# Output rows in token order, half chunks joined, and all output transfers small and on one queue

## The chip, the cores and the metric

The kernel runs on one core of a Trainium2 chip. A core has a matrix engine (TensorE, PE in the profile, with its weight loads as PEld), a vector engine (VectorE, DVE), a scalar engine (ScalarE, ACT), a general engine (GpSimd, POOL) and SyncE (SP), which here only issues transfers. Products land in PSUM; all other on-chip data lie in SBUF, 128 partitions wide. The metric is the device time of one launch in microseconds.

## What is computed

Linear attention with exponential features, then a layer that mixes the first 64 Fourier modes along the sequence, and a residual with a channel product:

```python
q, k, v: (8, 8, 576, 64);  w_phi: (64, 128)
def phi(x):
    proj = x @ w_phi
    proj = proj - max(abs(proj), axis=-1)
    return concat([exp(proj), exp(-proj)])
num = phi(q) @ (phi(k)^T v);  den = phi(q) . sum_s phi(k) + 1e-6
x = (num / den) as (8, 576, 512)                  # heads side by side

X = rfft(x, axis=1)[:, :64]
Y = X @ (w_r + i w_i)                             # per mode a 512 x 512 matrix
y = irfft(Y, n=576, axis=1)
u = x + y
out = u + relu(u @ w_ch)                          # float32
```

## The kernel before

**Tokens.** The 576 tokens of a batch are read as p and n, token = 9 p + n with 64 values of p and 9 of n. The kernel keeps them in five chunks c: partition 64 jj + p of chunk c holds token n = 5 jj + c, with jj = 0 or 1. Chunk 4 has only jj = 0, so half of its 128 rows mean nothing. The attention result x is xs_all, one 128x512 block per batch and chunk, index i = 5 b + c.

**Two stages.** The first (up to L605) runs the attention, 32 steps, and beside it the mode products as their weights arrive: 32 groups k of 8 modes by 128 rows (the first eight cut otherwise), two loads each, wr and wi, of which three groups' buffers exist (pool pw, tags w0 and w1). The last ten groups, k = 22 to 31, run after the attention, in the loop of L685. The loads are issued by GpSimd, each when the buffer of three groups earlier is free.

In that loop a group does mode_mm (L382), mode_sum (L416), a transpose (ptY) into sY, and for every second group by_batch (L660): from sY it makes z = Y w_ch (psZ, PSUM tag T0) and a reordered Y (psR, tag T1) for 32 of the 128 mode rows. Four copies per by_batch then spread both over zall and yall by batch (copy(j), L676: batches j and j + 4; ScalarE for zall, VectorE for yall). They are queued in the list copies and taken out one by one between other work. pieces(n) (L648) fills in n times: flip_x transposes two blocks of xs_all (tag T3) into sT, times_w multiplies them by w_ch (tag T2) and ScalarE casts the result into xw. plan gives n for each k.

**The output units.** After the last group 20 units follow (L738 to L775). A unit is two blocks: two chunks of one batch, or chunk 4 of batches b and b + 4. chan (L710) adds xw through an identity and the inverse transform CI times zall in PSUM, and ScalarE takes the relu into the output tile. spec (L721) does CI times yall; VectorE adds it to the tile. The residual xs_all comes in either through one more identity product (ident_b), or, where a unit is called late, through an addition on GpSimd (L736). Eleven units are late: the four of chunk 4, and seven of the eight with chunks 0 and 1. Chunks and units go by batch: b and b + 4 for b = 0 to 3; for b = 3 the unit of chunk 4 comes first.

PSUM has four tags of two banks, T0 to T3. Units 0, 1 and 2 and all even units use T2 (chan) and T3 (spec), the others T0 and T1, which are free once the last by_batch's copies are done.

**Transfers.** For b < 3 an output tile of[x] leaves when its four chunks are done, as two transfers of 512 KB, partitions 0 to 63 (jj = 0) by SyncE and 64 to 127 (jj = 1) by ScalarE's queue two or three units later; for b = 3 there are two of 256 KB per unit. Chunk 4 leaves from partitions 0 to 63 of Yacc, one transfer of 256 KB in rows of 2 KB. That is 24 transfers, 9.44 MB.

The order on every engine is the order of the code (tc.manual_schedule), and each engine works through its own in sequence.

Of the kernel before, what the change touches and what calls it, by code (L numbers as in the profile page):

```python
# [10 lines left out]
F32 = mybir.dt.float32  # L11
F32R = mybir.dt.float32r
BF16 = mybir.dt.bfloat16
I32 = mybir.dt.int32
ACT = mybir.ActivationFunctionType
ALU = mybir.AluOpType
# [4 lines left out]
DMODEL = 512  # L21
NCH = 5
# [4 lines left out]
def kernel(  # L27
# [11 lines left out]
    nc = tc.nc  # L39

    const = ctx.enter_context(tc.tile_pool(name="const", bufs=1))
    pers = ctx.enter_context(tc.tile_pool(name="pers", bufs=1))
    psum_cm = tc.tile_pool(name="psum", bufs=1, space=bass.MemoryType.PSUM)
    psum = psum_cm.__enter__()
    pw = ctx.enter_context(tc.tile_pool(name="pw", bufs=3))

    ident_b = const.tile([128, 128], BF16, name="ident_b")

    XT1 = pers.tile([128, 80, NMODES], BF16, name="XT1")
    xs_all = pers.tile([128, B_ * NCH, DMODEL], BF16, name="xs_all")

    Yacc = pers.tile([128, 8, DMODEL], F32, name="Yacc")
# [7 lines left out]
    CI = const.tile([128, NCH, 128], BF16, name="CI")  # L62
# [9 lines left out]
    coefcol = pa_c.tile([128, 1], F32, name="coefcol")  # L72
# [420 lines left out]
    def inverse_matrix(c):  # L493


        if c == 0:
            make_identity(nc, ident_f)
            nc.vector.memset(coefcol, 2.0 / S_)
            nc.vector.memset(coefcol[0:2, :], 0.0)
            nc.vector.memset(coefcol[0:1, :], 1.0 / S_)  # L500
        pct = psum.tile([128, 128], F32, name="pct", tag="tx", bufs=1)
        nc.tensor.transpose(pct, trig[:, c, :, :].rearrange("p m r -> p (m r)"), ident_f)
        nc.vector.tensor_scalar_mul(out=CI[:, c, :], in0=pct, scalar1=coefcol)

    psY = None
    k_in = k_out = 0
# [2 lines left out]
    with tc.manual_schedule():  # L509
# [15 lines left out]
        for n in range(N + 2):  # L525
# [60 lines left out]
            e = n - (N + 2 - N_EARLY)  # L586
# [10 lines left out]
            if 10 <= n < 10 + NCH:  # L597
                inverse_matrix(n - 10)
# [16 lines left out]
    psum = ctx.enter_context(tc.tile_pool(name="psumT", bufs=1, space=bass.MemoryType.PSUM))  # L615
# [4 lines left out]
    yall = pb.tile([128, B_, DMODEL], BF16, name="yall", bufs=1)  # L620
    zall = pb.tile([128, B_, DMODEL], BF16, name="zall", bufs=1)
# [3 lines left out]
    todo = list(range(N_EARLY, B_ * NCH, 2))  # L625
    ahead = []
    copies = []
# [20 lines left out]
    def pieces(n):  # L648
        for _ in range(n):
            if todo:  # L650
                flip_x(todo.pop(0))
            if copies:
                copies.pop(0)()
            if len(ahead) > 1:
                times_w()
            if copies:
                copies.pop(0)()


    def by_batch(sY, P):  # L660
        cols = [sY[:, dc].rearrange("p g c -> p (g c)") for dc in range(4)]
        psZ = psum.tile([128, 2, DMODEL], F32, name="psZ", tag="T0")
        for h in range(2):
            for dc in range(4):
                for j in range(4):
                    nc.tensor.matmul(psZ[32 * j:32 * j + 32, h, :], lhsT=cols[dc][:, j + 4 * h::8],
                                     rhs=wchb[:, dc, :], start=(dc == 0), stop=(dc == 3))
        psR = psum.tile([128, 2, DMODEL], F32, name="psR", tag="T1")
        for h in range(2):
            for dc in range(4):  # L670
                for j in range(4):
                    nc.tensor.matmul(
                        psR[32 * j:32 * j + 32, h, dc * 128:(dc + 1) * 128],
                        lhsT=cols[dc][:, j + 4 * h::8], rhs=ident_b, start=True, stop=True)

        def copy(j):  # L676
            r = slice(32 * j, 32 * j + 32)
            nc.scalar.copy(zall[32 * P:32 * P + 32, j::4, :], psZ[r])
            nc.vector.tensor_copy(yall[32 * P:32 * P + 32, j::4, :], psR[r])

        copies.extend([lambda j=j: copy(j) for j in range(4)])

    with tc.manual_schedule():
        plan = {22: 3, 23: 3, 24: 2, 25: 2, 26: 2, 27: 1, 28: 2, 29: 1, 30: 1, 31: 0}
        while k_out < 32:  # L685
            k = k_out
            gi = groups[k][1]
            while k_in < min(k_out + NW, 32):
                weights(k_in)
                k_in += 1  # L690
            yst = mode_sum(k, mode_mm(k, "T3"), pb)
            k_out += 1
            if yst is not None:
                if ahead:
                    times_w()
                pt = psum.tile([128, 4, 128], BF16, name="ptY", tag="T3")
                for dc in range(4):
                    nc.tensor.transpose(pt[:, dc, :], yst[:, dc * 128:(dc + 1) * 128], ident_b)
                if gi % 2 == 0:
                    sY = pb.tile([128, 4, 2, 128], BF16, name="sY", tag="sY")  # L700
                nc.vector.tensor_copy(sY[:, :, gi % 2, :], pt)
                if gi % 2 == 1:
                    by_batch(sY, gi // 2)
            pieces(plan[k])
            if k == 30:
                times_w()
        assert not todo and not ahead and len(copies) == 4


    def chan(u):  # L710
        ps = psum.tile([128, 2, DMODEL], F32, name="psB", tag=u["tags"][0])
        for x, (b, c) in enumerate(u["bc"]):
            i = b * NCH + c
            nc.tensor.matmul(ps[:, x, :], lhsT=ident_b,  # L714
                             rhs=xw0[:, i, :] if i < N_EARLY else xw[:, i - N_EARLY, :],
                             start=True, stop=False)
            nc.tensor.matmul(ps[:, x, :], lhsT=CI[:, c, :], rhs=zall[:, b, :],  # L717
                             start=False, stop=True)
        nc.scalar.activation(u["o"], ps, ACT.Relu)

    def spec(u):  # L721
        ps = psum.tile([128, 2, DMODEL], F32, name="psA", tag=u["tags"][1])
        for x, (b, c) in enumerate(u["bc"]):
            i = b * NCH + c
            if not u["late"]:
                nc.tensor.matmul(ps[:, x, :], lhsT=ident_b, rhs=xs_all[:, i, :],
                                 start=True, stop=False)
            nc.tensor.matmul(ps[:, x, :], lhsT=CI[:, c, :], rhs=yall[:, b, :],  # L728
                             start=u["late"], stop=True)
        o = u["o"]  # L730
        nc.vector.tensor_tensor(out=o, in0=ps, in1=o, op=ALU.add)  # L731
        if u["late"]:
            (b, c), (b1, c1) = u["bc"]
            i0 = b * NCH + c
            di = b1 * NCH + c1 - i0
            nc.gpsimd.tensor_tensor(out=o, in0=o, in1=xs_all[:, i0:i0 + di + 1:di, :], op=ALU.add)  # L736

    units = []  # L738
    for b in range(4):
        last = b == 3  # L740
        of = [pw.tile([128, 4, DMODEL], F32, name="of", tag=f"w{x}") for x in range(2)]
        o4 = Yacc[:, 2 * b:2 * b + 2, :]
        us = []
        for x in range(2):
            out_v = out[b + 4 * x].rearrange("(p n) e -> p n e", n=9)
            for c in (0, 2):
                dmas = []
                if last or c == 2:
                    c0 = c if last else 0
                    dmas = [(out_v[:, 5 * jj + c0:5 * jj + c + 2, :],  # L750
                             of[x][64 * jj:64 * jj + 64, c0:c + 2, :]) for jj in range(2)]
                us.append(dict(bc=((b + 4 * x, c), (b + 4 * x, c + 1)), o=of[x][:, c:c + 2, :],
                               late=c == 0 and not (last and x == 1), dmas=dmas))
        u4 = dict(bc=((b, 4), (b + 4, 4)), o=o4, late=True,
                  dmas=[(out[b::4].rearrange("x (p n) e -> p x n e", n=9)[:, :, 4, :], o4[0:64])])
        units += [u4] + us if last else us + [u4]

    with tc.manual_schedule():

        LAG = 3  # L760
        copies.pop(0)()
        for n in range(len(units) + LAG):
            if copies:
                copies.pop(0)()
            if n < len(units):
                u = units[n]
                u["tags"] = ("T2", "T3") if n % 2 == 0 or n < 3 else ("T0", "T1")
                chan(u)
                spec(u)
                for dst, src in u["dmas"][0:1]:  # L770
                    nc.sync.dma_start(dst, src)
            for lag, late in ((2, False), (3, True)):
                if 0 <= n - lag < len(units) and units[n - lag]["late"] == late:
                    for dst, src in units[n - lag]["dmas"][1:2]:
                        nc.scalar.dma_start(dst, src)  # L775


# [28 lines left out]
```

## Time and profile before

| | |
|---|---|
| median of three runs | 466.02 us (464.96 to 467.11) |
| the profiled execution | 464.41 us, of which the profile's span is 462.6 |
| PE, DVE, ACT, POOL busy | 306.8, 300.0, 255.6, 199.0 us |
| issue of the last weight load (wi) | before 387.69 us, used by PE at 415.48 |
| first and last output transfer issued on SP | 427.02 and 457.0 us |
| last add on DVE | 453.29 to 454.51 us |
| output transfers on SP | 10 from of, 467 / 494 / 1367 ns to issue (least, median, most); 4 from Yacc, 621 / 622 / 647 |
| output transfers on ACT's queue | 10, 474 / 506 / 812 ns |
| relu (ACT), add (DVE), residual add (POOL) of a unit | 1.02, 1.22 and 2.13 us |

Times in the profile are microseconds from the start of the span. A line of the order of instructions has start, duration, engine, source line, operation, what it writes and reads, and in brackets how long the engine had been idle and for whom. A line of the stage windows has busy time and number of instructions for PE, PEld, DVE, ACT and POOL, then the granted clock of PE as a share of full, the DMA engines' share and their rate in GB/s. SPq and ACTq are the issues of transfers on SyncE and ScalarE.

### The profile page before, as it was taken

The page shows a single profiled execution, that of the slowest core. Times are in us where ns is not written, and L with a number is a line of the kernel's source. Part 1 is how long each engine was busy: PE and PEld are TensorE (multiplying, and loading weights), DVE is VectorE, ACT ScalarE, POOL GpSimd, SP SyncE. Part 2 cuts the span into 40 slices and gives each one's busy share as a digit, 9 for nine tenths or more (in the row PEclk, how much of TensorE's full clock was granted, in tenths as well). Part 3 has the DMA queues.
Part 4 walks back from the last instruction along what each step waited for, and adds up shares of the span by engine and source line. Part 5 has one row for each costly group of instructions (what it writes and reads, how often), then busy time and mean ns, then how long its engine had stood idle before and what let it go on. Part 6 is the DMA issues. An engine that isn't in the chain of part 4 may idle for free.

```text
span 462.6 us, 11028 instructions
## 1 busy us (share of the span) xinstructions
PE 306.8 (66%) x4598; PEld 203.3 (44%) x4615; DVE 300.0 (65%) x417; ACT 255.6 (55%) x519; POOL 199.0 (43%) x247
## 2 busy tenths in 40 slices
PE   1575777655677686656465655666577887577991
PEld 1364665543454565534343443444344444333440
DVE  5678789854988788866555564765333456437882
ACT  3765786743676877755555453656122434336671
POOL 4596486545564356644344333433021131001782
PEclk9997798976787859997677787998999999979997
DMA  8999999999999999999999999999999999970997
GB/s 189 252 249 246 245 185 218 228 206 222 216 226 219 229 218 229 218 227 221 218 208 228 208 218 219 208 206 209 206 207 207 207 207 207 207 133 1 232 317 269
DMA packets 83553, 99.08 MB, mean 214 GB/s; under 512 B 3248, under 2 KB 75568, under 8 KB 82736
## 3 DMA queue, kind: packets, MB, share of 16 engines
q0 software_dynamic: 73872, 74.72, 97.1%
q1 hardware_dynamic: 8672, 19.40, 14.0%
q10 hardware_dynamic: 960, 4.26, 2.9%
q8 instruction: 36, 0.59, 0.5%
q14 instruction: 13, 0.11, 0.1%
HBM read 163.64 MB, written 9.44 MB: 374 GB/s over the span
## 4 chain that ended last, share of the span: by engine, by line
DMA 32%; DVE 22%; issue 19%; PE 14%; POOL 5%; ACT 4%; SPq 1%; DVEq 0%; ACTq 0%; POOLq 0%
DMA wi<-in_moe_w_i_dram 19%; DVE mkq L225 7%; DMA wr<-in_moe_w_r_dram 7%; DMA q<-in_q_dram 4%; DVE xs_all L328 4%; DVE nd L314 3%; DVE tB L307 3%; DMA kn<-in_k_dram 2%; PE ptr L176 2%; ACT AA L232 2%; PE psNB L297 2%; PE psB L714 2%; PE psA L728 2%; PE psB L717 2%; POOL vaug L262 2%
## 5 line engine op out<-in xcount | busy, mean ns | idle before, releaser
L262 POOL TENSOR_TENSOR vaug<-vn,ee 128x576 bf16<-128x576 f32 x64 | 72.6, 1152 | 59.7 <-ACT ee L247 53.1
L232 ACT ACTIVATE AA<-psT 128x1024 bf16<-128x1024 f32 x64 | 62.0, 1021 | 44.4 <-PE psT L200 43.9
L154 POOL DMA_DIRECT2D wr<-in_moe_w_r_dram x24 | 21.8, 908 | 111.4 <-PE psY L408 105.5
L254 ACT ACTIVATE e<-mkq 64x4 f32<-64x4 f32 (+1 forms) x128 | 26.3, 206 | 66.1 <-DVE mkq L225 61.8
L236 ACT ACTIVATE AA<-psk 128x1024 bf16<-128x1024 f32 x64 | 61.3, 1008 | 0.0
L408 PE MATMUL psY<-wi,XT 128*32 128x512 bf16 x192 | 24.2, 452 | 31.3 <-DMA wi<-in_moe_w_i_dram 31.3
L646 ACT CAST xw<-psW 128x1024 bf16<-128x1024 f32 x17 | 17.2, 1012 | 48.1 <-PE psW L644 48.1
L408 PEld LDWEIGHTS <-XT 128*32 128x32 bf16 x384 | 17.9, 167 | 57.5 <-issue 49.7
L225 DVE TENSOR_REDUCE mkq<-psk 128x8 f32<-128x1024 f32 x32 | 38.7, 1211 | 0.7 <-PE psk L191 0.7
L225 DVE TENSOR_REDUCE mkq<-psq 128x8 f32<-128x1024 f32 x32 | 38.9, 1216 | 0.2
L427 DVE TENSOR_TENSOR Yacc<-psY,Yacc 128x512 f32<-128x512 f32 x16 | 11.0, 688 | 41.7 <-PE psY L408 41.7
L644 PE MATMUL psW<-wchb,sT 128*128 128x512 bf16 x127 | 33.2, 393 | 3.7 <-ACT xw L646 2.1
L278 PE MATMUL kvz<-vaug,AA 64*128 64x65 bf16 x1152 | 30.4, 214 | 6.3 <-POOL vaug L267 5.1
L182 DVE COPY kT<-ptr 128x640 bf16<-128x640 bf16 x32 | 15.7, 491 | 29.1 <-PE ptr L176 29.1
L408 PE MATMUL psY<-wr,XT 128*32 128x512 bf16 x192 | 23.8, 451 | 16.1 <-DMA wr<-in_moe_w_r_dram 6.3
L307 DVE TENSOR_TENSOR tB<-psNB,e 128x650 f32<-128x650 f32 x32 | 26.7, 833 | 10.9 <-PE psNB L297 10.3
L297 PEld LDWEIGHTS <-AA 128*128 128x128 bf16 x640 | 30.4, 113 | 7.6 <-issue 6.9
L328 DVE TENSOR_TENSOR xs_all<-nd,rden 128x640 bf16<-128x640 f32 x32 | 31.1, 970 | 1.1
L736 POOL TENSOR_TENSOR of<-of,xs_all 128x1024 f32<-128x1024 f32 x7 | 14.9, 2132 | 39.0 <-DVE of L731 38.8
L278 PEld LDWEIGHTS <-AA 64*128 64x128 bf16 x1152 | 26.1, 110 | 11.3 <-issue 7.6
L200 PE MATMUL psT<-qT,w 64*128 64x512 bf16 x64 | 15.7, 482 | 21.3 <-DVE mkq L225 21.2
L314 DVE TENSOR_TENSOR nd<-psNA,tB 128x650 f32<-128x650 f32 x32 | 26.7, 835 | 3.8 <-DVE tB L307 0.5
(120 smaller groups left out, 722.8 us busy)
## 6 DMA issues: line engine op xcount, KB each, us to landing
wr<-in_moe_w_r_dram POOLq DMA_DIRECT2D x24, 1024.0 KB, 24.3
wi<-in_moe_w_i_dram POOLq DMA_DIRECT2D x24, 1024.0 KB, 28.4
wr<-in_moe_w_r_dram POOLq DMA_DIRECT2D x16, 512.0 KB, 17.6
wi<-in_moe_w_i_dram POOLq DMA_DIRECT2D x16, 512.0 KB, 20.7
vn<-in_v_dram SPq DMA_DIRECT2D x24, 288.0 KB, 5.6
q<-in_q_dram POOLq DMA_DIRECT2D x12, 288.0 KB, 19.3
k<-in_k_dram POOLq DMA_DIRECT2D x12, 288.0 KB, 19.4
out_dram<-of SPq DMA_DIRECT2D x6, 512.0 KB, 6.0
```

What stands on the lines that cost most here:

```text
L225: nc.vector.tensor_reduce(out=o, in_=i, axis=AX.X, op=ALU.max, apply_absolute_value=True)
L232: nc.scalar.activation(AA[:, 0, ab, 0:1024].rearrange("f (x j p) -> f j x p", j=2, p=64), st["psT"].rearrange("f j (x p) -> f j x p", p=64 ...
L236: nc.scalar.activation(AA[:, 1, ab, 0:1024].rearrange("p (c j f) -> p j c f", c=4, j=2), st["psk"], ACT.Exp, scale=sc)
L254: nc.scalar.activation(e2[64 * jj:64 * jj + 64, hh, 0:NCH - jj], mkq[64 * hh:64 * hh + 64, 1, 5 * jj:5 + 4 * jj], ACT.Exp, scale=2.0)
L262: nc.gpsimd.tensor_tensor(out=vaug[:, ab, :, 0:64], in0=st["v"], in1=ee[:, ab, :].unsqueeze(2).to_broadcast([128, 9, D_]), op=ALU.mult,)
L278: nc.tensor.matmul(kvz[:, hh, ab * 65:(ab + 1) * 65], lhsT=AA[r, 1, ab, 128 * j:128 * j + 128], rhs=vaug[r, ab, j, :], start=(j == 0), sto ...
L297: nc.tensor.matmul(p[:, hh, 65 * c:65 * c + 65], lhsT=AA[:, 0, ab, x:x + 128], rhs=kvzF[:, hh, ab * 65:(ab + 1) * 65], start=True, stop=True,)
L307: nc.vector.tensor_tensor(out=tB, in0=st["psNB"], in1=e2.unsqueeze(3).to_broadcast([128, 2, NCH, 65]), op=ALU.mult,)
L314: nc.vector.tensor_tensor(out=nd, in0=st["psNA"], in1=st["tB"], op=ALU.add)
L328: nc.vector.tensor_tensor(out=xo, in0=nd[:, :, :, 0:64], in1=rden.to_broadcast([128, 2, NCH, 64]), op=ALU.mult,)
L408: nc.tensor.matmul(psY[32 * j:32 * j + 32, :], lhsT=XT[:, c0:c0 + 32, m], rhs=wt[ri][:, 2 * j + par, :], start=(par == 0 and ri == 0), sto ...
L644: nc.tensor.matmul(ps[:, x, :], lhsT=sT[:, x, dc, :], rhs=wchb[:, dc, :], start=(dc == 0), stop=(dc == 3))
```

## The change

1. **Token order.** A second identity, ident_p, has its columns in the order (p, jj) instead of (jj, p), and the columns of CI for chunks 0 to 3 are written in that order too. So the products of an output unit give row 2 p + jj. The identity products of xw and xs_all use ident_p.
2. **In place for late units.** Ten pairs of blocks of xs_all, those of the new late units, are put in the new order in place by reordered: two products with ident_p into tag T0 or T1 and one ScalarE copy back. It is called up to twice after pieces for k up to 24 and for even k after that, once the pair has been transposed by flip_x.
3. **Half chunks joined.** Chunk 4 of batches b and b + 4 now fills partitions 0 to 63 and 64 to 127 of one 128x512 tile, through products with 64 columns. These units are no longer late. The late units are (batch half x, chunk) as listed in late.
4. **Last by_batch.** For the last one the products are split by half h, and copies has five entries: half 0's products and copy of batch 0, the same for half 1 and batch 4, then copies 1, 2 and 3, the last with both casts on ScalarE. One is taken before the units and one after each of the next units (before: one ahead of each).
5. **Tags.** Units 0 to 4 use T2 and T3 (before: 0 to 2, and 4).
6. **Transfers.** Every unit has two transfers, partitions jj, jj + 2, ... of its own two chunks (256 KB, rows of 4 KB), or for the joined half chunks one per batch (128 KB, rows of 2 KB): 40, all by SyncE; a unit that isn't late at once, a late one two units later, ahead of that step's own.

```diff
+            nc.vector.tensor_copy(ident_p.rearrange("r (p j) -> r j p", j=2),
+                                  ident_b.rearrange("r (j p) -> r j p", j=2))
...
-        nc.vector.tensor_scalar_mul(out=CI[:, c, :], in0=pct, scalar1=coefcol)
+        o, i = CI[:, c, :], pct
+        if c < 4:
+            o, i = o.rearrange("r (p j) -> r j p", j=2), i.rearrange("r (j p) -> r j p", j=2)
+        nc.vector.tensor_scalar_mul(out=o, in0=i, scalar1=coefcol)
...
+    late = {0: ((1, 0), (1, 2)), 1: ((0, 0), (1, 0), (1, 2)), 2: ((0, 0), (1, 0), (1, 2)),
+            3: ((0, 0), (0, 2))}
+    reorder = sorted((b + 4 * x) * NCH + c for b in range(4) for x, c in late[b])
+
+    def reordered(tag):
+        i = reorder[0]
+        if todo and i + 2 > todo[0]:
+            return
+        reorder.pop(0)
+        ps = psum.tile([128, 2, DMODEL], F32, name="psX", tag=tag)
+        for x in range(2):
+            nc.tensor.matmul(ps[:, x, :], lhsT=ident_p, rhs=xs_all[:, i + x, :],
+                             start=True, stop=True)
+        nc.scalar.copy(xs_all[:, i:i + 2, :], ps)
...
-        copies.extend([lambda j=j: copy(j) for j in range(4)])
+        if P < 3:
+            for f in (mm_z, mm_r):
+                for h in range(2):
+                    f(h)
+            copies.extend([lambda j=j: copy(j) for j in range(4)])
+        else:
+
+            copies.extend([lambda: (mm_z(0), mm_r(0), copy(0, 0)),
+                           lambda: (mm_z(1), mm_r(1), copy(0, 1)),
+                           lambda: copy(1), lambda: copy(2), lambda: copy(3, None, True)])
...
             pieces(plan[k])
+            if k <= 24 or k % 2 == 0:
+                assert not copies
+                for tag in ("T0", "T1"):
+                    if reorder:
+                        reordered(tag)
...
+    def parts(u):
         for x, (b, c) in enumerate(u["bc"]):
+            if u["half"]:
+                yield slice(64 * x, 64 * x + 64), 0, b, c, ident_b[:, 0:64], CI[:, c, 0:64]
+            else:
+                yield slice(0, 128), x, b, c, ident_p, CI[:, c, :]
...
-                               late=c == 0 and not (last and x == 1), dmas=dmas))
+                               late=(x, c) in late[b], half=False,
+                               dmas=[(out_v[:, 5 * jj + c:5 * jj + c + 2, :],
+                                      of[x][jj::2, c:c + 2, :]) for jj in range(2)]))
+        u4 = dict(bc=((b, 4), (b + 4, 4)), o=o4, late=False, half=True,
+                  dmas=[(out[b + 4 * x].rearrange("(p n) e -> p n e", n=9)[:, 4, :],
+                         o4[64 * x:64 * x + 64]) for x in range(2)])
...
-        LAG = 3
+        LAG = 2
         copies.pop(0)()
         for n in range(len(units) + LAG):
-            if copies:
-                copies.pop(0)()
             if n < len(units):
                 u = units[n]
-                u["tags"] = ("T2", "T3") if n % 2 == 0 or n < 3 else ("T0", "T1")
-                chan(u)
+                u["tags"] = ("T2", "T3") if n % 2 == 0 or n < 4 else ("T0", "T1")
+                add_xw(u)
+                add_z(u)
                 spec(u)
-                for dst, src in u["dmas"][0:1]:
-                    nc.sync.dma_start(dst, src)
-            for lag, late in ((2, False), (3, True)):
-                if 0 <= n - lag < len(units) and units[n - lag]["late"] == late:
-                    for dst, src in units[n - lag]["dmas"][1:2]:
-                        nc.scalar.dma_start(dst, src)
+                if copies:
+                    copies.pop(0)()
+            for lag, is_late in ((LAG, True), (0, False)):
+                if 0 <= n - lag < len(units) and units[n - lag]["late"] == is_late:
+                    for dst, src in units[n - lag]["dmas"]:
+                        nc.sync.dma_start(dst, src)
```

## The prediction

> **What bounds the kernel now.** I read the slices first, then the chain of waits, then the stage windows, then the order of instructions. The slices (40 of 11.6 us) show two stages. Up to the 36th the DMA row stands at 9 and moves some 207 GB/s; then come one slice of nothing and three of output.
>
> ```profile
> DMA  8999999999999999999999999999999999970997
> GB/s 189 252 249 246 245 185 218 228 206 222 216 226 219 229 218 229 218 227 221 218 208 228 208 218 219 208 206 209 206 207 207 207 207 207 207 133 1 232 317 269
> q0 software_dynamic: 73872, 74.72, 97.1%
> ```
>
> The chain of waits from 410 us on names the weight load that ends the first stage; the stage windows (PE, PEld, DVE, ACT, POOL busy, clock, DMA share, GB/s) show what follows it.
>
> ```profile
> 387.69 27.75 DMA wi<-in_moe_w_i_dram
> 385.00:405.00 20.00, 12.83 (x154) 7.59 (x156) 12.18 (x14) 7.90 (x8) 1.75 (x2) 0.99 1.24 207
> 415.00:427.00 12.00, 8.31 (x102) 4.27 (x99) 7.45 (x9) 7.34 (x8) 2.13 (x1) 1.00 0.01 1
> 433.00:435.00 2.00, 1.95 (x10) 0.90 (x10) 1.93 (x2) 1.30 (x2) 2.00 (x2) 1.00 1.03 205
> 437.00:461.00 24.00, 16.00 (x74) 7.08 (x73) 14.57 (x12) 11.26 (x11) 14.70 (x7) 0.89 0.93 309
> 457.00:459.00 2.00, 0.00 (x0) 0.00 (x0) 0.00 (x0) 0.00 (x0) 0.00 (x0) 0.50 0.99 358
> ```
>
> The reader sees: to 415 us weights bound it and PE has a third of its time free. From 415 to 427 DMA is idle while the last group is turned into the first output unit. From 427 the engines and the output transfers run side by side. In 433 to 435 DMA is fully busy yet moves 205 GB/s; in 457 to 459, as busy, 358. The packet records explain it: 8 KB packets take 628 ns when only one 64-partition half is in flight and 309 ns when both are.
>
> The last instructions in order of time show that the compute is over well before the end:
>
> ```profile
> 453.29 1.22 DVE L731 TENSOR_TENSOR of<-psA,of 128x1024 f32<-128x1024 f32 x1 [0.45 <-ACT of L719]
> 453.60 4.41 SPq L771 DMA_DIRECT2D out_dram<-of  x4
> 452.29 4.75 ACTq L775 DMA_DIRECT2D out_dram<-of  x4
> ```
>
> The last add ends at 454.51, the last transfer is issued at 457.0 and its bytes end near 461.5: some 3.5 us of the end is backlog. So compute and drain both weigh on the tail, and nothing before 415 does.
>
> **Step 1, reordering in the last groups: +0.45 us.** Ten calls of reordered, each two 128x512 products (0.22 us each, from 0.38 x 39 pipelined at 0.2157 apart in the chain) and one ACT copy of 1.01 (the row of L646, same shape). Nine fall at k = 22 to 28, under the weight loads: PE is busy 12.8 of 20 us there and ACT 7.9, and 9 x 0.43 us PE and 9 x 1.01 us ACT are spread over some 70 us. Loads are not delayed: a weight takes 24 to 28 us from issue to landing, and a group of 2.1 MB at 207 GB/s ten, so the queue always holds more than two groups. Without that cover they would cost up to 9 x 1.44 = 13 us. The tenth, at k = 30, sits just before the last group, where the cover is thin:
>
> ```profile
> 411.48 2.02 ACT L678 CAST zall<-psZ 32x1024 bf16<-32x1024 f32 x2
> 412.76 1.90 PE L644 MATMUL psW<-wchb,sT 128*128 128x512 bf16 x8 [0.79 <-DVE sT L636]
> 415.48 0.48 PE L408 MATMUL psY<-wi,XT 128*32 128x512 bf16 x4 [0.42 <-DMA wi<-in_moe_w_i_dram]
> ```
>
> Its products wait in tag T0 for those two casts (413.5), end at 413.98, and only then may the eight of L644 start: 413.98 + 1.73 = 415.7. The sixteen of the last group then end at 416.83 and not 416.39. Bounds: 0 (a free PE) and 1.0 (0.43 plus a clock at half for a moment, as in the 0.68 granted from 405 to 415). ident_p and the scattered CI columns (342 ns a copy, L503) lie under the loads: nothing.
>
> **Step 2, the first unit: first output 3.8 us earlier.** The last by_batch is split. sY is ready at 418.05 + 0.45 = 418.5. Sixteen z-products are half of 1.96 (418.09 to 420.05): 0.98. The cast of 32x512 costs 0.59 (ACT L380, 128x512, 586 ns), not 1.00. Then what is left of the identity products, two CI products and latency (0.6), relu 1.02 and add 1.23, with some 0.3 of hand-overs: the add ends at 423.2. Unit 0 is not late, so SyncE issues at once, against 427.02 now.
>
> **Step 3, units 1 to 4: the lead is lost.** Tags stay T2/T3 up to unit 4 (before: up to 2), so each unit waits for the add before it, and DVE alternates a yall cast (1.22) and an add (1.23): adds end at 426.2, 428.7, 431.2 and, a half unit of 0.69 (L427's shape), 432.7. Now they end at 424.4, 426.9, 429.5, 430.8, 432.5. Copy 3 puts a second cast on ACT (+1.0) ahead of the fourth relu, and PE waits behind unit 4's spec, which needs the third add. Unit 5 starts on PE at 431.7 and its add ends at 435.1 instead of 433.8: 1.3 us late.
>
> **Step 4, units 5 to 19: PE gets 2.6 us back.** Now these fifteen take 8 x 6 + 7 x 8 = 104 products; then 8 x 6 + 4 x 8 + 3 x 4 = 92 slots, if the 64-column pairs of a half unit run together, as L345's 128x64 ones do (20 of 256 columns in 1.28 us, two abreast 1.07). 104 - 92 = 12 x 0.2157 = 2.6 us. ACT and DVE halve on half units too (0.59, 0.69), but two in a row (14 and 15) have PE wait for the adds of 12 and 13, which gives back about 1.2. Last add: 431.7 + 88 x 0.2157 + 1.2 stall + 0.2 + 1.02 + 1.23 = 454.4, as now. If the pairs don't run together: 456.2. GpSimd does ten adds of 2.13 instead of eleven; unit 17's ends at 454.45.
>
> **Step 5, the drain: -2.5 us.** SyncE alone issues 40 transfers (now 24 on two queues). One costs 494 ns median (L771); pairs on SP at the start take 1.10 together, so 0.55 each. At step n = 19 SyncE first waits for unit 17 (454.45), and unit 19's add is queued behind that: four issues, done at 456.7. The data: 5.5 MB belong to the twelve units from unit 9's issue on (first byte 442.9). The rate is unknown. Low bound 309 GB/s, the mean now from 437 to 461; high bound 351, from the final 4 KB packets now (187 ns mean on 16 engines: 16 x 4096 / 187). The new transfers are 4 KB rows whose 64 partitions are spread over all 128, nearest to the latter: I take 340. 5.5 / 0.340 = 16.2, so 459.1, and about 0.4 of gaps: 459.5. By 309 it is 460.8, by 351 459.3. Bytes now end at 461.5 and the span at 462.6, so the new span is 459.5 + 1.1 = **460.6: -2.0 us**.
>
> [...] The row is 205 against 358 GB/s at full DMA share. [...]
>
> **Against the runs.** The profiled execution took 464.41 for a span of 462.6; the median is 466.02. I carry the difference over: 466.02 - 2.0 = **464.0**.
>
> **Rivals.** (a) *The start does not slip.* If the hand-overs of step 3 pack tighter, the 1.3 us stay, the last add ends near 453.1 and the bytes at 458.2: -3.3, 462.7. For it: the fourth add now follows the third without a gap (428.24, 2.53 us for two). Against: that one uses T0/T1, which the new code keeps shut until unit 5.
>
> (b) *The strided halves collide; slower.* The double time that a lone half shows (628 ns per 8 KB) could stay with every second partition on one queue; then the drain decides from unit 2's issue (431) on. Put through the same list of issues, bytes end at 461.4 at 300 GB/s, which is even with now: that is the point. At 267 the time is past the mark; at 250 bytes end at 465.7, span 466.8, time 470.2; at 209 throughout 472.1, time 476.6. For it: one queue, and 203 GB/s from 427 to 437 now. Against: 75% of the last 4 KB packets took full speed with halves mixed.
>
> (c) *SyncE's issues bound, or the pairs don't run abreast.* At 0.70 an issue, as SP and ACT show at the end while both press (8 in 5.7 us), bytes end at 461.4; with unpaired halves 461.2. Either way the span is 462.3 to 462.5: no change, 465.8.
>
> (d) *The reorders stall the weight stage.* One exposed reorder is 1.44; two or three more of them exposed make the time 466.9 to 468.3.
>
> **Chances.** Forecast 0.45, (a) 0.22, (b) 0.18, (c) 0.09, (d) 0.06. Half a per cent, 2.3 us, is about what can be told from no change. The forecast's own range is 462.4 to 465.6, of which a third is past the mark. Faster: 0.14 + 0.22 = 0.36. Slower: 0.17 of (b), 0.08 of (c) and (d) = 0.25. Same: 0.39. The range over all: low 461.0 (a, and a rate of 358 with no gaps), high 470.5 (b at 250).
>
> **What would show it.** Step 1: the last group's products end 0.4 to 0.5 us after the last weight's landing would have them. Step 2: first output issue near 423. Step 3: fourth add at 432 to 433. Step 4: half units take 0.86 us of PE, last add near 454. Step 5: issues of about 0.55 on SP, the last near 456, 4 KB packets near 187 ns. Wrong if packets average above 220 ns (b), or if the last add lies over 1.5 us from 454.4.

## The result, and the profile after

| | before | after |
|---|---|---|
| median | 465.78 us (464.96 to 467.11, 5 runs) | 461.76 us (461.70 to 463.58, 5 runs) |
| the same, beside the experiments | 465.47 us (35 runs) | 462.95 us (461.56 to 466.91, 12 runs) |
| profiled execution, span | 464.41, 462.6 us | 463.39, 461.6 us |

The ratio is 0.9927, 95% interval [0.9899, 0.9955], and beside the experiments 0.994 [0.9907, 0.9973]: the change makes the kernel 0.6 to 0.7% faster, some 3 us. The forecast was 464.0, 2.0 us less than before; these medians differ by 4.0 us, those beside the experiments by 2.5. The first median after, 461.76, lies just under the forecast's own range (462.4 to 465.6), the second, 462.95, within it. The two profiled executions differ by only 1.0 us; why that is less than the medians' difference comes below.

The slices of after (the DMA engines' share, the rate), its SP queue and its issues:

```profile
DMA  8999999999999999999999999999999999981488
GB/s 170 262 254 241 237 218 217 229 206 219 221 225 218 229 218 222 221 223 224 218 208 223 213 218 219 207 208 207 207 207 207 207 207 207 207 140 63 146 318 293
q1 hardware_dynamic: 10496, 23.60, 15.7%
out_dram<-of SPq DMA_DIRECT2D x32, 256.0 KB, 2.4
```

The weight stage is as it was, 207 GB/s up to the same slice. Behind it output now starts one slice earlier, and a transfer lands 2.4 us after its issue; before it took 4.7 to 6.6 in the median. The stage windows of after (PE, PEld, DVE, ACT, POOL busy, clock, DMA share, GB/s):

```profile
423.00:425.00 2.00, 1.75 (x9) 0.70 (x8) 0.84 (x2) 1.86 (x2) 0.00 (x0) 1.00 0.65 262
430.50:434.00 3.50, 3.50 (x11) 1.08 (x11) 0.69 (x1) 1.08 (x2) 2.12 (x1) 0.52 0.51 181
437.00:454.50 17.50, 16.70 (x85) 6.89 (x83) 13.35 (x14) 11.70 (x13) 14.58 (x8) 1.00 0.80 286
457.00:459.00 2.00, 0.00 (x0) 0.00 (x0) 0.00 (x0) 0.00 (x0) 0.00 (x0) 0.70 1.00 402
```

Look at the rate in the last window: with the DMA engines full, 402 GB/s flow, where the same window of before had 358. Up to 454 the share is 0.80, so the DMA has slack and the compute sets the pace. And for 3.4 us from 430.5 the clock of PE is at half. The order of instructions of after, first and last add, and the last eight issues:

```profile
421.08 1.23 DVE L786 TENSOR_TENSOR of<-psA,of 128x1024 f32<-128x1024 f32 x1 [1.39 <-ACT of L773]
454.36 1.23 DVE L786 TENSOR_TENSOR of<-psA,of 128x1024 f32<-128x1024 f32 x1 [0.45 <-ACT of L773]
453.50 4.99 SPq L824 DMA_DIRECT2D out_dram<-of  x8
```

The first add ends at 422.3 instead of 424.4, yet the last ends at 455.6 instead of 454.5. The gain is not in the adds.

The packet records give one more measure that the rest uses: **the tail**, from the start of the last weight packet to the end of the span. That packet comes at another time in each profile (413.6 to 417.3 us over all that follow), which moves a whole execution by up to 3.7 us; kernels that are alike up to there differ by as much, so it isn't the change.

### The profile page after: what moved, and what is told of

Same layout as the page of the kernel before. It is cut to its first block, busy times and chain, and to the rows that moved or that the text cites. A ratio compares the mean times of both kernels' runs of the same rounds, so it can differ in the third digit from the quotient of the medians.

```text
span 461.6 us, 11115 instructions
## 1 busy us (share of the span) xinstructions
PE 312.4 (68%) x4637; PEld 202.2 (44%) x4637; DVE 298.8 (65%) x418; ACT 264.5 (57%) x531; POOL 196.3 (43%) x246
## 4 chain that ended last, share of the span: by engine, by line
DMA 26%; DVE 25%; issue 19%; PE 16%; ACT 6%; POOL 5%; SPq 2%; DVEq 0%; ACTq 0%; POOLq 0%
DMA wi<-in_moe_w_i_dram 20%; DVE mkq L227 7%; DVE xs_all L330 4%; DMA q<-in_q_dram 4%; DVE nd L316 3%; DVE tB L309 3%; ACT AA L234 3%; PE psNB L299 2%; ACT e L256 2%; PE ptr L178 2%; DVE of L786 2%; SPq L123 2%; DMA kn<-in_k_dram 2%; PE psB L764 1%; POOL vaug L264 1%
## 5 line engine op out<-in xcount | busy, mean ns | idle before, releaser
L410 PE MATMUL psY<-wi,XT 128*32 128x512 bf16 x192 | 25.3, 472 | 25.5 <-DMA wi<-in_moe_w_i_dram 25.5
L790 POOL TENSOR_TENSOR of<-of,xs_all 128x1024 f32<-128x1024 f32 x10 | 21.1, 2130 | 42.2 <-DVE of L786 42.2
L654 ACT CAST xw<-psW 128x1024 bf16<-128x1024 f32 x17 | 17.2, 1013 | 36.4 <-PE psW L652 36.4
L652 PE MATMUL psW<-wchb,sT 128*128 128x512 bf16 x136 | 32.2, 379 | 2.1 <-ACT xw L654 2.1
L178 PE MATMUL ptr<-ident_b,k 128*128 128x128 bf16 x160 | 18.4, 263 | 17.2 <-DVE qT L184 16.5
```

The source lines that it names most:

```text
L410: nc.tensor.matmul(psY[32 * j:32 * j + 32, :], lhsT=XT[:, c0:c0 + 32, m], rhs=wt[ri][:, 2 * j + par, :], start=(par == 0 and ri == 0), sto ...
L652: nc.tensor.matmul(ps[:, x, :], lhsT=sT[:, x, dc, :], rhs=wchb[:, dc, :], start=(dc == 0), stop=(dc == 3))
```

## The experiments

Medians of 10 to 12 runs (7 for the second filled run), with ratios to the kernel before on the same chip. Packets are the mean time of the 4 KB ones (8 KB where 4 KB ones are only the last eight transfers').

| run | median us | ratio [95%] | packets ns | tail us |
|---|---|---|---|---|
| changed kernel | 462.95 | 0.994 [0.9907, 0.9973] | 162 | 46.9 |
| contiguous halves | 468.6 | 1.0074 [1.0045, 1.0102] | 220 | 52.5 |
| no reordering | 463.14 | 0.9922 [0.9892, 0.9953] | 162 | 46.6 |
| filled, first try | 465.7 | 1.0003 [0.9974, 1.0031] | 162 | 49.0 |
| by_batch in one piece | 462.32 | 0.9924 [0.9894, 0.9955] | 162 | 45.8 |
| two queues | 464.4 | 0.9963 [0.9932, 0.9993] | 165 | 46.3 |
| filled, second try | 462.16 | 0.9911 [0.9876, 0.9946] | 162 | 45.3 |
| one tile for half units | 461.63 | 0.9916 [0.9883, 0.9949] | 162 | 44.9 |
| whole transfers | 463.5 | 0.9967 [0.9939, 0.9994] | 318 (8 KB) | 45.6 |
| contiguous, two queues | 467.71 | 1.0073 [1.0041, 1.0105] | 219 | 49.9 |
| contiguous, whole | 470.11 | 1.0077 [1.0045, 1.0109] | 494 (8 KB) | 54.5 |

The kernel before had 456 ns for 8 KB packets, and tails of 47.5 and, in a second profile, 50.0 us.

The distance from the end of the last add to the end of the span tells the two causes of a long tail apart. In the nine profiles with every second partition it is 5.9 to 6.3 us: the end follows the adds. In the kernel before it is 8.1 and 8.4, in the three contiguous runs 12.0, 7.2 and 13.3 (in the order of the table): there a backlog of transfers is left when the adds are done.

**The changed kernel again.**

> The changed kernel once more, for a second profile. Two groups of spans were seen, 460.0 and 461.7 us. Theory A (the clock): the slower group has PE granted half speed for 3.4 us from about 430.5, after PE idles 1.4 us before unit 4's products; a profile in the fast group shows 1.00 there and its last add near 453.9, one in the slow group shows the half and 455.6. Rival (weights): the groups differ in when the last weight lands, and the last add stands equally far behind it in both.

The second profile, from a slower execution (466.0), has the half clock too, 3.4 us from 433.4, and the same tail to 0.1 us (47.0). What differs is the last weight packet: 417.3 instead of 414.7. So the rival holds for these two: the executions differ by when the weights land.

**Contiguous halves.**

```diff
-                yield slice(0, 128), x, b, c, ident_p, CI[:, c, :]
+                yield slice(0, 128), x, b, c, ident_b, CI[:, c, :]
...
-        if c < 4:
+        if False:
...
-    reorder = sorted((b + 4 * x) * NCH + c for b in range(4) for x, c in late[b])
+    reorder = []
...
-                                      of[x][jj::2, c:c + 2, :]) for jj in range(2)]))
+                                      of[x][64 * jj:64 * jj + 64, c:c + 2, :]) for jj in range(2)]))
```

> The changed kernel with the old token order: halves leave from partitions 0 to 63 and 64 to 127 again, and nothing is reordered; still 40 small transfers by SyncE. Theory A: the gain of the change lies in the spread over the partitions; packets of 4 KB go back from 162 ns to over 200 on average, backlog returns, bytes end 2 to 4 us later, 463.5 to 466. Rival B: the gain is the earlier start and the small transfers; time stays within 1 us of 461.8, or falls by the saved reordering.

5.7 us slower than the changed kernel, and slower than the kernel before. Its windows of ten microseconds:

```profile
437.00:447.00 10.00, 9.52 (x52) 3.88 (x52) 8.32 (x8) 6.84 (x8) 8.46 (x5) 1.00 0.83 230
447.00:457.00 10.00, 6.06 (x27) 2.53 (x27) 5.59 (x5) 4.10 (x4) 6.52 (x4) 1.00 0.82 265
```

The same windows of the changed kernel:

```profile
437.00:447.00 10.00, 9.82 (x53) 4.09 (x52) 7.94 (x8) 7.01 (x8) 8.11 (x5) 1.00 0.72 268
447.00:457.00 10.00, 6.89 (x34) 2.80 (x31) 6.49 (x7) 4.69 (x5) 7.53 (x4) 1.00 0.91 328
```

With the halves contiguous a larger share (0.83 against 0.72) moves less (230 against 268), so a backlog builds. The last add ends at 454.6, a microsecond earlier than in the changed kernel's profile; the bytes end at 465.0, five later than there. Theory A holds, and by more than it said (468.6, against 463.5 to 466).

**No reordering.** `reorder = []` alone.

> The changed kernel without the ten calls of reordered (the late units' residual rows are then added in the old order). Theory: all ten lie under the weight loads, the time stays within 0.5 us of the changed kernel's (461.3 to 462.3). Rival, from the prediction: the tenth delays the last group by 0.45 us, and with more of them exposed the time falls by 1.4 us each.

463.14 against 462.95: ten reorderings cost nothing that can be measured, but these medians could not show 0.45 us either; the profiles can. In this run PE waits for the last weight longer than in the changed kernel, by about what the reordering takes there, which is what cover looks like. The order of PE's instructions in this run:

```profile
415.14 0.48 PE L410 MATMUL psY<-wi,XT 128*32 128x512 bf16 x4 [2.95 <-DMA wi<-in_moe_w_i_dram]
```

And in the changed kernel:

```profile
411.53 0.59 PE L679 MATMUL psX<-xs_all,ident_p 128*128 128x512 bf16 x2 [1.36 <-ACT zall L705]
411.96 1.89 PE L652 MATMUL psW<-wchb,sT 128*128 128x512 bf16 x8
415.01 0.48 PE L410 MATMUL psY<-wi,XT 128*32 128x512 bf16 x4 [0.75 <-DMA wi<-in_moe_w_i_dram]
```

The wait for T0 (1.36 us) is there as foreseen, but 0.75 us of waiting for the weight are left behind it. Over all profiles, the first product that uses the last weight starts 0.30 to 0.38 us after the end of its last packet, with reordering or without, except in two with it (filled, first try, and one tile), where it starts 0.5 us after: there PE came to it only then. So the tenth reordering costs nothing or 0.2 us.

The wait that it fills is not free of cost either: in this profile the clock of PE is at half from 417.4 to 420.8 us, behind that wait, and the first add ends 6.05 us after sY instead of 4.73. No run shows how often that happens.

**Filled, twice.** Six products into the unread half of unit 4's PSUM tile; the first time after the relu in the order of the code, the second time ahead of it. The second edit:

```diff
+        if u is units[4]:
+            for _ in range(6):
+                nc.tensor.matmul(ps[:, 1, :], lhsT=ident_b, rhs=xw[:, 0, :], start=True, stop=True)
         nc.scalar.activation(u["o"], ps[:, 0, :] if u["half"] else ps, ACT.Relu)
```

> The changed kernel with six products more, written to an unread half of unit 4's PSUM tile while PE would wait for the third add (no result changes). Theory A: PE stays busy, the half clock after 430.5 is gone, all runs lie with the fast group or below it, 460.5 to 461.8. Rival: the half clock comes regardless or was not the cause, and the two groups remain, 461.7 and 463.5.

> Six products more as in the run before, now ahead of unit 4's relu so that they fill PE's idle stretch (with them PE would be busy some 2.8 of the 3.4 us before 430.5, not 1.5). Theory A: a 3.4 us stretch with little PE work is followed by 3.4 us at half clock; with the stretch filled the half clock after 430 is gone, unit 5's add comes 1.5 us earlier against the last weight, and the time falls by about 1.5 us to 461.5. Rival: the half clock comes from something else and stays; the time is that of the changed kernel, 462.9.

The first try failed by its own design: the products waited 1.92 us for the relu (they write the tile that it reads), began only at 430.1, and the half clock came at 430.6 all the same, so that they took 2.34 us of path. The second filled the gap, and its profile has no half clock there and a tail of 45.3. But the profiles of the run in one piece, of two queues and of whole transfers have none either, without any filling, so this run doesn't show that the filling took it away; its median of 462.16 can't be told from the changed kernel's. What the profiles do show is when the half clock comes. In each of them the granted clock changes only at multiples of 3.413 us from some first moment, which differs from profile to profile (in the first profiles of before and after the 35 and 43 distances between one change and the next are whole multiples of it to within 0.01 us, the shortest 3.413 us); such a stretch between two possible changes is called a grid window here. The next lines are the windows before a half clock (to within 0.06 us), PE's busy time first. In the changed kernel:

```profile
427.08:430.50 3.42, 1.45 (x10) 0.38 (x8) 3.28 (x3) 3.29 (x5) 2.12 (x1) 1.00 0.22 87
```

In its second profile:

```profile
430.00:433.40 3.40, 1.48 (x10) 0.48 (x9) 2.95 (x3) 3.35 (x4) 2.43 (x2) 1.00 0.13 51
```

And in the first filled run:

```profile
427.20:430.60 3.40, 1.48 (x9) 0.46 (x8) 2.29 (x2) 2.83 (x4) 3.01 (x2) 0.99 0.07 29
```

In all three PE is busy for 1.45 to 1.48 of 3.4 us. The fourteen profiles have 199 grid windows between 400 us and the last add that are at full clock themselves. In eleven of them PE is busy for 1.52 us or less, and each of these is followed by a half clock; in the other 188 it is busy for 1.63 us or more, and none of these is. The first profile of before has 13 of these windows: 0.47 us of work in the one ahead of a half clock, 2.01 or more in the others; that of after has 14, with 1.45 us and 1.87 or more. The window closest to the bound that kept the clock, and the next one, in the run with by_batch in one piece:

```profile
407.41:410.82 3.41, 1.63 (x14) 0.91 (x14) 2.79 (x3) 2.71 (x4) 0.00 (x0) 1.00 0.92 152
410.82:414.23 3.41, 1.89 (x15) 0.86 (x17) 0.35 (x1) 1.56 (x2) 0.00 (x0) 1.00 0.38 63
```

And PE's standing still before unit 4's second product in the contiguous run, as long as in the changed kernel (1.37 us) but in a window with more work beside it:

```profile
429.70:433.11 3.41, 2.04 (x13) 0.84 (x11) 1.98 (x3) 2.26 (x4) 3.02 (x2) 1.00 0.38 77
433.11:436.52 3.41, 3.41 (x17) 1.57 (x16) 2.45 (x2) 2.44 (x3) 1.58 (x2) 1.00 0.89 270
```

So in these profiles it goes with where those 1.4 us fall on the grid whether the next 3.4 us run at half speed: 1.45 us of PE work in the window ahead of the half clock, 2.04 ahead of the full one. In the second filled run they fall in a window that holds 3.42 us of PE work, or some 1.9 without the six products (1.47): estimated from the windows above, the clock would have stayed at full without them too. No run forced the half clock either way, and the bound is that of this late part: between 60 and 400 us, where PE has other products, windows with up to 1.70 us of work in before (from 87.2 us) and 1.81 in the changed kernel (from 147.2 us) were followed by a half clock, and one with 1.52 in before (from 326.1 us) was not.

**By_batch in one piece.** The branch for P == 3 removed, four copies, the last with both casts on ScalarE.

> The changed kernel with the last by_batch in one piece again (all products first, then four copies, one before the units and one after each). Theory A: the first add and first issue come later by about 1 us (0.98 of products and 0.4 of a wider cast), the second by less, and the end is set by PE and the issues, so the time stays within 0.7 us of the changed kernel's 462.9. Rival: the early start is worth what it shows at the front, and the time rises by 1 to 1.5 us.

From sY's end the first add takes 6.0 us instead of 4.7, and the time is 462.32: the earlier first unit is not what the gain is made of. The theory holds; of 1.3 us at the front 0.4 are left at unit 5 (its add ends 17.2 us after sY, against 16.8 in the second filled run).

**Two queues.** The jj = 1 transfers by ScalarE, one step later.

```diff
+            for jj, eng, lags in ((0, nc.sync, ((LAG, True), (0, False))),
+                                  (1, nc.scalar, ((LAG + 1, True), (1, False)))):
...
```

> The changed kernel with the jj = 1 transfers on ScalarE's queue, one unit later than on SyncE's. Theory A: at the end SyncE issues eight transfers back to back in 5.0 us while the DMA moves 402 GB/s, so both are full and a second queue brings nothing: within 0.5 us of the changed kernel (462.4 to 463.4). Rival B: the issues are the bound, the last falls 1 to 2 us earlier and the time by as much, 461 to 462. Rival C: the issues on ScalarE hold up the relus and it is slower, 464 or more.

464.4 is in the range of C, though the ratios (0.9963 against 0.994) don't separate it from the changed kernel. The profile agrees with both A and C: from the last add to the end it is 5.9 us, as with one queue (6.0), so a second queue brings nothing at the end; and the last add comes 37.5 us after sY, against 36.4 in the second filled run. One relu that is held up: behind the two half units (14 and 15) ScalarE runs no relu for 1.94 us instead of 1.23, with two issues of transfers in that time.

**One tile for half units.** Both products of a joined half unit in the two halves of its first tile, so that the second doesn't wait for tag T3.

```diff
+        if u["half"]:
+            for r, x, b, c, idn, ci in parts(u):
+                nc.tensor.matmul(ps[r, 1, :], lhsT=idn, rhs=xs_all[:, b * NCH + c, :],
+                                 start=True, stop=False)
+            for r, x, b, c, idn, ci in parts(u):
+                nc.tensor.matmul(ps[r, 1, :], lhsT=ci, rhs=yall[:, b, :], start=False, stop=True)
...
+            nc.vector.tensor_tensor(out=o, in0=u["psB"][:, 1, :], in1=o, op=ALU.add)
```

> The changed kernel with a joined half unit's second product in the free half of its first PSUM tile, so that it doesn't wait for the add before it. Theory A: PE no longer stands still before unit 4's second product (1.4 us) nor at units 14 and 15 (about 1.2 us), and the half clock goes too: last add 2.5 to 4 us earlier against the last weight, time 459.5 to 461. Rival: the drain and the issues hold the end, and the time falls by less than 1 us (462 to 463).

The order of PE's instructions in this run, at unit 4's second product (the first two lines) and the start of unit 5:

```profile
428.11 0.38 PE L775 MATMUL psB<-xs_all,ident_b 128*64 128x512 bf16 x2
428.32 0.38 PE L778 MATMUL psB<-yall,CI 128*64 128x512 bf16 x2
428.66 0.59 PE L764 MATMUL psB<-xw,ident_p 128*128 128x512 bf16 x2
```

And at unit 6:

```profile
430.92 0.59 PE L764 MATMUL psB<-xw,ident_p 128*128 128x512 bf16 x2 [0.75 <-DVE Yacc L784]
```

From unit 4 PE goes straight on into unit 5, which ends its add 15.6 us after sY instead of 18.1, and the last add comes 35.9 after sY, not 38.0 (16.8 and 36.4 in the second filled run, which has no half clock there). The tail is the shortest of all, 44.9. The median of 461.63 beats the kernel before (0.9916 [0.9883, 0.9949]); against the changed kernel it is better by about a microsecond that these runs can't separate. That is between theory A and the rival, and not for the rival's reason: from the last add to the end it is 6.0 us, as in the changed kernel and in the second filled run, so the drain takes nothing of what the adds gain. Of the 1.2 us that unit 5 is ahead of the second filled run most is lost one unit later, where PE waits 0.75 us for the half unit's add (the last line), and 0.5 are left at the last add.

**Whole transfers.** Chunks 0 to 3 leave together for the first three batch pairs, every second partition as in the change.

> The changed kernel with the transfers of the first three batch pairs kept whole again (four chunks, two of 512 KB in rows of 8 KB, when the tile is complete), still every second partition and all by SyncE. Theory A: what counts is the spread over the partitions; the DMA runs at some 400 GB/s and is partly free up to 441, the last eight transfers are as before, so the time stays within 1 us of the changed kernel's (462 to 464). Rival: the early small transfers are worth their 4.7 us at the front, and the time rises by 2 us or more (465 and up).

463.5: theory A. Early and small pieces are worth 0.6 us by the medians and 0.3% by the ratios (0.994 against 0.9967), which these runs can't separate from nothing, though output now starts 3 us later against sY. 8 KB packets take 318 ns, against 456 in the kernel before: the spread works at both sizes.

**The kernel before again.**

> The kernel before, for a second profile. In its first profile the span ends 47.5 us after the last weight packet, with 8 KB packets at 456 ns on average; the changed kernel's ends 47.0 after it with a half clock in between and 45.4 without. Theory A: the tail repeats to within 1 us and the runs differ by when the last weight lands (413.5 to 417.2 seen). Rival: the first profile was a lucky one, and the tail is 49 or more.

The tail is 50.0 us, not 47.5: the rival. PE's clock is at half from 416.2 to 423.0 there, just when the last group turns into the first unit, and sY to first add takes 7.8 us instead of 6.4:

```profile
416.20:423.00 6.80, 5.70 (x49) 2.21 (x52) 1.12 (x2) 0.00 (x0) 0.00 (x0) 0.50 0.01 2
```

It comes behind a wait of 2.92 us for the last weight, in a grid window with 0.85 us of PE work. The first profile of before came from an execution 1.4 us under its median (464.41 against 465.78), this one from one 2.8 us above that of its chip (468.0 against 465.17), so neither is typical. The profile of after, with its half clock, is 1.6 us above its median (463.39 against 461.76). That is why the first profiles differ by 1.0 us and the medians by 4.0.

**Contiguous, two queues and whole.** The contiguous run with the edit of two queues, and with that of whole transfers.

> The old token order as in the contiguous run (468.6), with the jj = 1 halves on ScalarE's queue one unit later, so that both halves are in flight together. Theory A: the contiguous halves cost that much because on one queue they follow each other and each uses half of the way out; with two queues 4 KB packets fall from 220 ns to below 200, and the time falls by 2 us or more, to 464.5 to 466.5. Rival: two queues on the same engines change nothing, packets stay at 220 ns and the time at 468.

> The old token order as in the contiguous run (468.6), and the transfers of the first three batch pairs whole again (two of 512 KB, rows of 8 KB), all by SyncE. Open: why the contiguous run is 3 us slower than the kernel before although its units are done as early. Theory A: small contiguous pieces are what costs, and whole ones bring the time back to that of the kernel before, 465 to 466. Rival: contiguous halves one after the other on one queue cost it at any size, and the time stays at 467.5 to 469.5.

Both rivals hold: 219 ns and 467.71, and 470.11, above the rival's range on a chip where the kernel before takes 466.8 (ratio 1.0077). That each half uses half of the way out is an estimate that fits the 628 and 309 ns of the kernel before, but not these 219 ns with both halves in flight. Neither brings back the time of before. Between 437 and 447 us the contiguous run moves 230 GB/s, with two queues 266, with whole transfers 252, and the kernel before, which has both, 305. That fits two small gains that add up, but a run with both and the rest of the change was not made; why the contiguous run is 3 us slower than before stays open. Nor was the spread alone, or the joining of half chunks alone, put into the kernel before.

Taken in pairs, the spread over every second partition is worth about the same in every form of transfer: 0.994 against 1.0074, 0.9963 against 1.0073 on two queues, 0.9967 against 1.0077 in whole transfers. That is 1.1 to 1.3%, some 5 to 6 us; without it the rest of the change loses 0.7%.

## Why the prediction was right, and where not

The sign and the place were right: a tail set by units and drain, nothing ahead of it, and most of the gain in the drain. Before, the end stood 8.1 us behind the last add; the sum made that 6.2, and it is 6.0. The number is in part luck, because two things that the sum left out have opposite signs: a half clock in both profiles of the changed kernel, and a base profile better than the median. The sum gave a tail of 460.6 - 415.1 = 45.5 us. The changed kernel's own two profiles show 46.9 and 47.0; those without a half clock in the tail show 45.3 to 46.3 where order and number of the units are those of the change. The terms, one by one:

- **Step 1 (+0.45) was wrong.** The wait for T0 took place, but the path was the weight, with 0.75 us to spare; the cover that looked thin was thin because PE had been at half clock in that profile (0.68 granted from 405 to 415): in the second profile of before PE waits 2.92 us for the same weight, not 0.42. Measured: nothing, or 0.2 us in two profiles.
- **Step 2 was right.** From sY to the first add 4.7 us were worked out and 4.7 measured.
- **Step 3 was right in its mechanism.** From sY, adds 1 to 4 end at 7.8, 10.3, 12.8 and 14.8 us; worked out were 7.7, 10.2, 12.7 and 14.2. The lead is lost by the fourth add (12.8; before 12.7). Not foreseen was the half clock that follows the same standing still in this profile (0.52 granted from 430.5 to 434): unit 5 ends 18.1 us after sY instead of 16.6.
- **Step 4 was right.** Without the half clock the last add comes 36.4 us after sY (second filled run; 35.9 worked out). The half units' pairs do run abreast: in the run with one tile the next pair starts 0.21 us later (428.11, 428.32), where a pair of 128 columns takes 0.43.
- **Step 5 was mis-sized on both sides.** "I take 340" GB/s, with 351 as the high bound: measured are 402, 4 KB packets at 162 ns. The two bounds were added up wrongly: with the same 0.4 us of gaps they are 461.1 (309 GB/s) and 459.0 (351), not 460.8 and 459.3. An issue costs 0.62, not 0.55 (4.99 us for eight). The two errors cancel: from the last add to the end of the span 6.2 us were worked out and 6.0 measured.
- **What the spread is worth was misjudged.** The sum has it only in the rate of the drain (340 GB/s, -2.5 us). Against the kernel before the net gain is of that size, some 3 us, but in the contiguous run, which lacks only the spread and the reordering, all of the gain is gone: the spread brings 1.1 to 1.3%, and the rest of the change costs 0.7%. Which part of the rest costs it, no run shows, nor why contiguous halves are slower; measured are 220 ns for their 4 KB packets against 162. Both halves in flight on two queues bring the contiguous run hardly anything (219 ns, and 467.71 us against 468.6), while the 8 KB packets of the kernel before took 628 ns in the median with one half in flight and 309 with both.
- **Rival (b)** falls: 4 KB packets are uniform, 159 to 166 ns on average in every two microseconds of the drain. **Rival (c)** falls in its price: issues do press at the end, eight in 5.0 us, but at the rate that the DMA takes (2.1 MB in 5.0 us are 420 GB/s, against 402 measured). **Rival (d)** falls with step 1. **Rival (a)** did not happen in the changed kernel; the run with one tile is what it would look like.
- **The base was off, and that helped.** The sum was made against a profile with a tail of 47.5 us, then carried to the median. A second profile has 50.0, from an execution slower than the median; against a tail between the two the change gains more than against the first.

## What to carry to other kernels

When 64 partitions are to leave, take every second one rather than one half: the order of the rows is the product's to choose and cost 0.2 us at most here, and packets fell from 220 to 162 ns. Before costing a tail from one profile, look at where the granted clock is at half, how far behind the last input the end stands, and how far behind the last add: between two executions of one kernel the tail moved by 2.5 us and the last input by 2.6, where the change is worth 3. A lead at the front of a chain is worth only what its busiest engine lets through: here VectorE, with a cast and an add per unit (3.28 of 3.42 us busy), gave back all of 1.7 us in four units.

## What was not expected of the hardware

- With every second partition and one queue, output reached 399 to 402 GB/s over two microseconds (418 with 8 KB packets, 443 to 445 us in the run with whole transfers). Contiguous halves reached 299 on one queue, 338 on two and 301 whole, the kernel before 358. Over ten microseconds from 437 and 447 the contiguous runs had 230 to 273, the changed kernel 268 and 328.
- In these profiles the granted clock changed only on a grid of 3.413 us. Late in the kernel a grid window with 1.52 us or less of PE work was followed by half clock, eleven times of eleven, in the changed kernel with no longer standing still than 1.37 us within the window; with 1.63 us or more it never was, in 188.
- The last weight packet came at 414.7 and 417.3 us in two executions of the changed kernel, and at 415.1 and 416.2 in two of the one before, after the same loads.
